# Loads of V, A's K, output weights and x cut into 16 source elements of 16 KB

## The chip, the cores and the metric

One core of a Trainium2 chip, the other cores idle. The metric is the time of one execution on the device in microseconds (us). A run is called slow when it is over 1.5% above the fastest of the same kernel; ratios are of fast runs alone, each made on one chip beside runs of the kernel before. Medians are of all runs of a kernel, and where a slow run is among them the text says so.

A few words: HBM is the chip's main memory, SBUF the core's own memory of 128 partitions. PE, DVE, ACT and POOL are the compute engines. A load (one DMA) is issued by a queue and carried out by 16 DMA engines in packets; the traces show small packets of 4 bytes with it, here called completions (14,112 for the 882 DMAs of the kernel before, 16 each), and the profile gives the time from issue to landing. In these traces a packet is as large as the piece that lies together in HBM (2 to 32 KB in the loads of these runs; the source element, here often called a row).

## The reference

Two attention blocks side by side, in bf16. Both have 16 sequences of 32 query tokens, model width 1024, 32 query heads of 128 and a cache of 1024 keys.

```python
# A: 4 KV heads, each shared by 8 query heads.  B: 32 KV heads, one for each query head.
q = (x @ wq).reshape(B, Sq, Hq, Dh).transpose(0, 2, 1, 3)
scores = einsum("bhqd,bhkd->bhqk", q, k) * Dh ** -0.5
p = softmax(scores)
o = einsum("bhqk,bhkd->bhqd", p, v)
y = o.transpose(0, 2, 1, 3).reshape(B, Sq, Hq * Dh) @ wo        # for A and for B
return concatenate([yA, yB], -1)
```

The caches of B are 128 MB each for K and V, those of A 16 MB each; the weights are 8 MB each. Nothing is read twice, so with x (1 MB each) 322 MB must come from HBM once; these are MB of 2^20 bytes, the profile counts them as 338 MB of 10^6.

## The kernel before

The work runs in 128 steps. Each loads one group of four B heads (1 MB of K in one DMA, 1 MB of V in four) and, every second step, one head of A's K and V (256 KB each). All DMAs are issued from one queue, that of SyncE (SP), in an order fixed ahead by a list scheduler in the kernel. Buffers are few (2 for B's K, 3 for B's V), so SP waits for a buffer and then refills it.

The four kinds of load that matter:

```python
def folded_load(e, dst, src):          # source and destination may have different shapes
    inst = ...(ins=e.lower_ap_dma(src), outs=e.lower_ap_dma(dst))     # one DMA, from SP's queue
    return e.add_instruction(inst)

# B's K: 128 rows of 8 KB to 128 partitions of 8 KB
ksrc = pb["k"][q.b, q.h0:q.h0 + 4].rearrange("a (p s) d -> (a p) (s d)", s=32)
e.dma_start(KB_sb[:, sl, :, :].rearrange("p i n -> p (i n)"), ksrc)

# B's V, one head: 32 source rows of 8 KB, each to 4 partitions of 2 KB
vsrc = pb["v"][q.b, q.h0 + t_].rearrange("(g p c) d -> g (p c d)", p=4, c=NCH)
folded_load(e, VB_sb[:, sl, t_, :, :].rearrange("p c d -> p (c d)"), vsrc)

# A's K (A's V, the output weights of one head, and x likewise): 128 rows of 2 KB to 128 partitions of 2 KB
e.dma_start(KA_sb[:, sl, :, :], pa["k"][q.b, q.s].rearrange("(p c) d -> p c d", c=NCH))

# projection weights: 2 x 128 pieces of 2 KB
e.dma_start(dst[:, k_ * jp:(k_ + 1) * jp, :], wq[...].rearrange("(j p) c -> p j c", p=P))
# ... compute, scheduler and stores left out
```

## Time and profile before

| | before |
|---|---|
| median of 3 runs, us | 850.37 (848.38 to 855.56) |
| span of the profiled run, us | 849.6 |
| PE / DVE / ACT busy | 85% / 64% / 53% |
| DMA, mean | 402 GB/s |

The page of the kernel before: the slice rows have 40 equal parts of the span, DMA is the busy share of the 16 DMA engines in tenths, GB/s what they moved. In the queue table come packets, MB and share of 16 engines' time. The last rows give the count of DMAs, KB of each, and median us from issue to landing.

```profile
span 849.6 us, 27817 instructions
...
DMA  9999999999999999999999999999999999999995
GB/s 346 384 389 404 410 397 398 414 403 391 411 414 417 417 409 415 414 382 403 419 414 415 412 417 418 409 411 417 419 420 415 407 417 419 408 390 410 418 413 195
DMA packets 82075, 341.59 MB, mean 402 GB/s; under 512 B 14112, under 2 KB 14624, under 8 KB 49184
...
q1 hardware_dynamic: 81952, 339.80, 99.3%
...
DMA 48%; PE 28%; DVE 12%; SPq 6%; issue 3%; ACT 2%; POOL 0%; POOLq 0%; DVEq 0%
...
KB_sb<-in_B_k_cache_dram SPq DMA_DIRECT2D x128, 1024.0 KB, 8.6
VB_sb<-in_B_v_cache_dram SPq DMA_DIRECT2D x512, 256.0 KB, 8.5
```

The DMA engines are busy nearly all the time (99.3%) and move some 415 to 420 GB/s in the good slices. The row before the last two is the chain that ended last: nearly half of it is DMA. The packet counts are cumulative: 14,112 small ones are the completions (16 for each of 882 DMAs), 34,560 have 2 KB, and the remaining 32,891 have 8 KB and more, among them 16,384 of B's K and 16,384 of B's V.

Who waits, in the kernel before (us in total, times, longest us):

```profile
DVE KBt_sb L844 <- DMA KB_sb<-in_B_k_cache_dram: 62.6, 67, 3.3
...
PE ps_o L971 <- DMA VB_sb<-in_B_v_cache_dram: 29.5, 27, 3.3
...
SPq L809 <- DVE KBt_sb L844: 101.2, 36, 7.7
```

The first two rows are compute that waits for data: little, for 850 us. The last is the issuing queue that waits for a free K buffer.

The packet records of the trace give each packet's duration: 84 ns (median) for 2 KB, 309 for 8 KB, 9 for a completion.

### The profile page before, as it was taken

How to read it: one execution, taken by the hardware profiler on the slowest of the kernel's cores; microseconds unless marked ns; L12 is line 12 of the kernel's file. 1: busy time of each engine (PE TensorE's matmuls, PEld its weight loads, DVE VectorE, ACT ScalarE, POOL GpSimd, SP SyncE). 2: the span in 40 equal slices, each digit the busy share in tenths (PEclk: the TensorE clock that was granted, in tenths of full speed). 3: DMA queues.
4: the chain of work that ended last, by engine and by line, in shares of the span. 5: the costliest groups of instructions: out<-in, count | busy, mean ns of one | idle time of the engine just before them, and what ended most of it. 6: DMA issues, size and time to landing. Idle time of an engine off the chain costs nothing.

```text
span 849.6 us, 27817 instructions
## 1 busy us (share of the span) xinstructions
PE 722.7 (85%) x12104; PEld 430.9 (51%) x12104; DVE 544.4 (64%) x1117; ACT 448.5 (53%) x981; POOL 68.2 (8%) x76
## 2 busy tenths in 40 slices
PE   3999999799988799789988788987999867877777
PEld 2556655456545455445654445553655544544443
DVE  0655676467755677457785566775677756757854
ACT  1455666366644466445655445754565635555453
POOL 0000000000000000000000000000000000000000
PEclk9999999999999999989999999999999989999999
DMA  9999999999999999999999999999999999999995
GB/s 346 384 389 404 410 397 398 414 403 391 411 414 417 417 409 415 414 382 403 419 414 415 412 417 418 409 411 417 419 420 415 407 417 419 408 390 410 418 413 195
DMA packets 82075, 341.59 MB, mean 402 GB/s; under 512 B 14112, under 2 KB 14624, under 8 KB 49184
## 3 DMA queue, kind: packets, MB, share of 16 engines
q1 hardware_dynamic: 81952, 339.80, 99.3%
q8 instruction: 96, 1.57, 0.7%
q14 instruction: 27, 0.22, 0.1%
HBM read 337.64 MB, written 2.10 MB: 400 GB/s over the span
## 4 chain that ended last, share of the span: by engine, by line
DMA 48%; PE 28%; DVE 12%; SPq 6%; issue 3%; ACT 2%; POOL 0%; POOLq 0%; DVEq 0%
DMA KB_sb<-in_B_k_cache_dram 28%; DVE KBt_sb L844 9%; DMA VB_sb<-in_B_v_cache_dram 8%; PE ps_pj L674 7%; DMA woB_sb<-in_B_wo_dram 6%; PE ps_s L879 5%; DMA VA_sb<-in_A_v_cache_dram 4%; SPq L498 4%; PE ps_pj L731 4%; PE ps_o L971 3%; PE ps_kt L937 2%; PE ps_pt L921 2%; PE ps_s L862 2%; DMA KA_sb<-in_A_k_cache_dram 1%; DMA acc<-in_B_x_dram 1%
## 5 line engine op out<-in xcount | busy, mean ns | idle before, releaser
L844 DVE STREAM_TRANSPOSE KBt_sb<-KB_sb 128x1024 f32<-128x1024 f32 x256 | 306.4, 1226 | 70.6 <-DMA KB_sb<-in_B_k_cache_dram 62.6
L902 ACT ACTIVATE P_sb<-ps_s 128x512 bf16<-128x512 f32 x256 | 151.8, 598 | 84.7 <-PE ps_s L879 73.7
L894 ACT ACTIVATE PTA_sb<-ps_s 128x1024 bf16<-128x1024 f32 x128 | 131.6, 1028 | 91.6 <-PE ps_s L862 73.7
L879 PE MATMUL ps_s<-KBt_sb,QB_sb 32*32 32x512 bf16 x4096 | 144.1, 388 | 9.4 <-DVE KBt_sb L844 4.6
L674 PE MATMUL ps_pj<-xT_sb,wq_sb 128*128 128x512 bf16 x448 | 121.0, 385 | 14.1 <-DMA wq_sb<-in_B_wq_dram 4.6
L818 POOL COPY VAp_sb<-VA_sb 128x1024 bf16<-128x1024 bf16 x64 | 66.7, 1042 | 762.3 <-DMA VA_sb<-in_A_v_cache_dram 735.8
L604 ACT COPY PT_sb<-ps_pt 128x512 f32<-128x512 f32 x128 | 75.0, 586 | 97.9 <-PE ps_o L971 80.6
L971 PE MATMUL ps_o<-VB_sb,PT_sb 128*32 128x128 bf16 x4096 | 82.3, 222 | 34.0 <-DMA VB_sb<-in_B_v_cache_dram 29.5
L921 PE MATMUL ps_pt<-id,P_sb 128*128 128x128 f32 x512 | 100.1, 302 | 8.5 <-ACT P_sb L902 5.7
L971 PEld LDWEIGHTS ps_o<-VB_sb,PT_sb 128*32 128x32 bf16 x4096 | 60.4, 97 | 71.4 <-issue 66.3
L921 PEld LDWEIGHTS ps_pt<-id,P_sb 128*128 128x128 f32 x512 | 79.4, 206 | 27.7 <-ACT P_sb L902 10.2
L862 PE MATMUL ps_s<-QT_sb,KTA_sb 128*128 128x256 bf16 x512 | 84.0, 275 | 7.3 <-ACT PTA_sb L894 5.1
L937 PE MATMUL ps_kt<-VAp_sb,PTA_sb 128*128 128x129 bf16 x1024 | 76.4, 221 | 7.9 <-ACT KTA_sb L604 2.6
L987 DVE TENSOR_SCALAR OB_sb<-ps_o,rinv_all 128x128 bf16<-128x128 f32 x128 | 44.0, 344 | 58.6 <-PE ps_o L971 57.2
L937 PEld LDWEIGHTS ps_kt<-VAp_sb,PTA_sb 128*128 128x128 bf16 x1024 | 64.4, 98 | 33.5 <-POOL VAp_sb L818 12.9
L879 PEld LDWEIGHTS ps_s<-KBt_sb,QB_sb 32*32 32x32 bf16 x4096 | 49.1, 89 | 62.2 <-issue 9.8
L731 PE MATMUL ps_pj<-woB_sb,OTB_sb 128*128 128x512 bf16 x240 | 68.2, 390 | 7.5 <-DMA woB_sb<-in_B_wo_dram 5.2
L674 PEld LDWEIGHTS ps_pj<-xT_sb,wq_sb 128*128 128x128 bf16 x448 | 40.3, 108 | 50.2 <-DMA wq_sb<-in_B_wq_dram 7.7
L742 DVE TENSOR_TENSOR acc<-acc,ps_pj 128x512 f32<-128x512 f32 x64 | 43.0, 672 | 30.4 <-PE ps_pj L731 30.2
L731 PE MATMUL ps_pj<-woA_sb,OTA_sb 128*128 128x512 bf16 x224 | 57.1, 379 | 3.7 <-DMA woA_sb<-in_A_wo_dram 1.9
L862 PEld LDWEIGHTS ps_s<-QT_sb,KTA_sb 128*128 128x128 bf16 x512 | 44.9, 98 | 29.0 <-ACT PTA_sb L894 9.1
L907 DVE TENSOR_TENSOR stat<-stat 64x1 f32<-64x1 f32 x256 | 41.9, 164 | 18.2 <-ACT P_sb L902 10.2
(52 smaller groups left out, 521.6 us busy)
## 6 DMA issues: line engine op xcount, KB each, us to landing
KB_sb<-in_B_k_cache_dram SPq DMA_DIRECT2D x128, 1024.0 KB, 8.6
VB_sb<-in_B_v_cache_dram SPq DMA_DIRECT2D x512, 256.0 KB, 8.5
KA_sb<-in_A_k_cache_dram SPq DMA_DIRECT2D x64, 256.0 KB, 9.2
VA_sb<-in_A_v_cache_dram SPq DMA_DIRECT2D x64, 256.0 KB, 8.8
wq_sb<-in_B_wq_dram SPq DMA_DIRECT2D x16, 512.0 KB, 10.3
woB_sb<-in_B_wo_dram SPq DMA_DIRECT2D x32, 256.0 KB, 9.8
woA_sb<-in_A_wo_dram SPq DMA_DIRECT2D x32, 256.0 KB, 8.7
wq_sb<-in_A_wq_dram SPq DMA_DIRECT2D x12, 512.0 KB, 10.0
```

Of the source, the lines that this page charges most:

```text
L604: pr.add("act", lambda e: e.copy(dst_ap, src_ap), reads=reads, writes=writes, name=name + "@act", wtag=wtag, rtag=rtag)
L674: last = e.matmul(ps_pj[:, 0:NTOK], pick(src, j), xT_sb[:, pi, j, :], start=(j == 0), stop=(j == DJ - 1))
L731: last = e.matmul(ps_a[:, 0:OUTW], OT[:, gp, hh, :], wo_[:, hh, oh * OUTW:(oh + 1) * OUTW], start=(hh == 0), stop=(hh == nh - 1))
L818: pr.add("pool", lambda g: g.tensor_copy(VAp_sb[:, sl, :, 0:Dh], VA_sb[:, :, :]), reads=["VA"], writes=[("VAp", sl)], name="VAp_cp", rtag= ...
L844: pr.add("dve", lambda e: e.transpose(KBt_sb[:, sl, t_, :].bitcast(F32).rearrange("p (s r i) -> p s r i", r=2, i=32), KB_sb[:, rs, t_, :]. ...
L862: last = e.matmul(ps_s[:, sbf, c2, i * 2 * P:(i + 1) * 2 * P], KTA_sb[:, sl, c * P:(c + 1) * P], qt, start=True, stop=True)
L879: last = e.matmul(ps_s[32 * cg:32 * cg + 32, sbf, g, :].rearrange("p (sh cl j) -> p sh cl j", sh=4, cl=4), lhsT, kt[32 * a:32 * a + 32, g, ...
L894: pr.add("act", lambda e: e.activation(dst, src, ACTF.Exp, scale=scale), writes=BK_S[sbf] + [("PTA", q.half)], name="expA", rtag={("Sv", s ...
L902: pr.add("act", lambda e, src=src, dst=dst, g=g: e.activation(dst, src, ACTF.Exp, scale=scale, accum_out=st[:, g:g + 1]), writes=[BK_S[sbf ...
L921: last = e.transpose(ps_pt32[:, m * P:(m + 1) * P], p32[:, m:Sk // 2:NPK], id32[:])
L937: last = e.matmul(ps_kt[:, qh * OA0:qh * OA0 + Dh + 1], PTA_sb[:, h, c, qh * P:(qh + 1) * P], VAp_sb[:, sl, 4 * h + c, 0:Dh + 1], start=(h ...
L971: last = e.matmul(ps_o[32 * a:32 * a + 32, 0:Dh], PT_pairs[:, c // 2, 32 * (a ^ (c // 4 * 2)):32 * (a ^ (c // 4 * 2)) + 32, c % 2], VB_sb[ ...
```

## The change

The intent: by estimate from the durations above a DMA packet has a fixed cost (5 ns, the remainder of 84 ns for 2 KB and 309 for 8 KB when what grows with the bytes and an overlap of 4 ns are taken off), so fewer and larger packets should move the same bytes in less time. Each 256 KB load becomes 16 source rows of 16 KB, so that each of the 16 DMA engines should get one packet. A row of 16 KB then fills 8 partitions of 2 KB.

```diff
-def folded_load(e, dst, src):
+def wide_load(e, dst, src, groups=16):
     ...
-        ins=e.lower_ap_dma(src), outs=e.lower_ap_dma(dst))
+        ins=e.lower_ap_dma(src.rearrange("(g n) d -> g (n d)", g=groups)), outs=e.lower_ap_dma(dst))
     return e.add_instruction(inst)
@@ x, output weights of A and of B, A's K, A's V: all in this way
-                e.dma_start(KA_sb[:, sl, :, :], pa["k"][q.b, q.s].rearrange("(p c) d -> p c d", c=NCH))
+                wide_load(e, KA_sb[:, sl, :, :].rearrange("p c d -> p (c d)"), pa["k"][q.b, q.s])
@@ B's V
-                    vsrc = pb["v"][q.b, q.h0 + t_].rearrange("(g p c) d -> g (p c d)", p=4, c=NCH)
-                    folded_load(e, VB_sb[:, sl, t_, :, :].rearrange("p c d -> p (c d)"), vsrc)
+                    vsrc = pb["v"][q.b, q.h0 + t_]
+                    wide_load(e, VB_sb[:, sl, t_, :, :].rearrange("p c d -> p (c d)"), vsrc)
```

B's K (8 KB packets) and the projection weights (2 KB) are not touched.

More of the change, by code (lines that the diff above doesn't have):

```diff
@@ L611, in xT_stage @@
             for tc in range(NG):
-                pr.add("sp", lambda e, tc=tc: e.dma_start(xst[:, tc, :], xfs[pi][tc * P:(tc + 1) * P, :]),
+                pr.add("sp", lambda e, tc=tc: wide_load(e, xst[:, tc, :], xfs[pi][tc * P:(tc + 1) * P, :]),
                        writes=accres if tc == 0 else [("xst", pi, tc)], reads=[] if tc == 0 else accres, dma_key=f"x{pi}_{tc}", name="x_dma", dur=P * D * 2)
@@ L700, in th @@
                 def th(h_=h_, r0=r0):
-                    pr.add("sp", lambda e: e.dma_start(woA_sb[:, h_, :], wo[r0:r0 + Dh, :]),
+                    pr.add("sp", lambda e: wide_load(e, woA_sb[:, h_, :], wo[r0:r0 + Dh, :]),
                            writes=[("woA", h_)], dma_key=f"woA{h_}", name="woA_dma", dur=Dh * D * 2, wtag={("woA", h_): s_})
@@ L710, in th @@
                 def th(h_=h_, r0=r0):
-                    pr.add("sp", lambda e: e.dma_start(woB_sb[:, h_, :], wo[r0:r0 + Dh, :]),
+                    pr.add("sp", lambda e: wide_load(e, woB_sb[:, h_, :], wo[r0:r0 + Dh, :]),
                            writes=[("woB", h_)], dma_key=f"woB{h_}", name="woB_dma", dur=Dh * D * 2, wtag={("woB", h_): m_})
@@ L803, in st_dmaK @@
                 sl = q.kvslot
-                pr.add("sp", lambda e: e.dma_start(KA_sb[:, sl, :, :], pa["k"][q.b, q.s].rearrange("(p c) d -> p c d", c=NCH)),
+                pr.add("sp", lambda e: wide_load(e, KA_sb[:, sl, :, :].rearrange("p c d -> p (c d)"), pa["k"][q.b, q.s]),
                        writes=[("KA", sl)], dma_key=f"ka{sl}", name="ka_dma", dur=Sk * Dh * 2, wtag={("KA", sl): q.kid})
@@ L815, in st_dmaV @@
                 sl = q.kvslot
-                pr.add("sp", lambda e: e.dma_start(VA_sb[:, :, :], pa["v"][q.b, q.s].rearrange("(p c) d -> p c d", c=NCH)),
+                pr.add("sp", lambda e: wide_load(e, VA_sb[:, :, :].rearrange("p c d -> p (c d)"), pa["v"][q.b, q.s]),
                        writes=["VA"], dma_key="va", name="va_dma", dur=Sk * Dh * 2, wtag={"VA": q.kid})
@@ L822, in st_dmaV @@
                 for t_ in range(4):
-                    vsrc = pb["v"][q.b, q.h0 + t_].rearrange("(g p c) d -> g (p c d)", p=4, c=NCH)
-                    pr.add("sp", lambda e, t_=t_, vsrc=vsrc: folded_load(e, VB_sb[:, sl, t_, :, :].rearrange("p c d -> p (c d)"), vsrc), writes=[("VB", sl, t_)],
+                    vsrc = pb["v"][q.b, q.h0 + t_]
+                    pr.add("sp", lambda e, t_=t_, vsrc=vsrc: wide_load(e, VB_sb[:, sl, t_, :, :].rearrange("p c d -> p (c d)"), vsrc), writes=[("VB", sl, t_)],
                            dma_key=f"vb{sl}_{t_}", name="vb_dma", dur=Sk * Dh * 2, wtag={("VB", sl, t_): q.kid})
```

## The prediction

> **What bounds the kernel now.** The DMA engines. DMA is at 9 tenths in 39 of 40 slices, the queue table gives the hardware queue 99.3% of 16 engines' span, at a mean of 402 GB/s. PE is busy 85%, DVE 64%, ACT 53%. The chain of waits is 48% DMA (B's K alone 28%), 28% PE, 12% DVE. Good slices run at 415 to 420 GB/s, poor ones at 380 to 400, where loads wait for buffers (waits of the issuing queue: 101 us on B's K transposes).
>
> **Where DMA time goes.** The packet records of the trace have three common durations: 84 ns for 2 KB (34,560 packets), 309 ns for 8 KB (32,768: half B's K, half B's V, already loaded in 8 KB source elements) and 9 ns for each 4-byte completion (14,112). Successive packets of one engine mostly overlap by 4 ns, so a packet costs about 80, 305 and 5 ns: 0.0366 ns per byte and 5 ns per packet. Summed over 16 engines this makes 803 us of 849.6; the rest is stretched packets (about 20 us), gaps, start and tail.
>
> **What the change does.** Instruction order, bytes, buffers and the count of DMAs stay. A load of 256 KB becomes 16 source elements of 16 KB, one per DMA engine. B's V: 16,384 packets of 8 KB to 8,192 of 16 KB. A's K and V, both output weights, x: 25,600 of 2 KB to 3,200 of 16 KB. Packets fall from 81,952 to about 51,360.
>
> Estimate from the durations above (16 KB: 605 ns effective, about 609 recorded): B's V saves 8,192 x 5 ns / 16 = 2.6 us; the 2 KB loads save (25,600 x 80 - 3,200 x 605) / 16 = 7.0 us. Together 9.6 us, 1.1%. [...]the trace agrees with a small fixed cost, here 5 ns, so most of it is already gone at 8 KB.
>
> **How much is on the critical path.** Nearly all in good slices, little in poor ones, where compute returns buffers late. I expect 60 to 100%: 6 to 9.6 us. Issuing a reshaped load takes 594 ns (B's V) against 432 ns for an ordinary one of the same size (timeline); some 200 such issues add 30 us, hidden behind 8 us of queued loads.
>
> **Prediction.** 842 us, 8 in 10 between 831 and 851. Faster by over 2%: 0.11; within 2%: 0.83; slower by over 2%: 0.06.
>
> **What the profile would show.** Packets near 51,400, almost all 2 KB packets left belonging to the projection weights; 16 KB packets at about 609 ns; good slices at 420 to 427 GB/s; PE, DVE and ACT busy times unchanged; poor slices still poor; DMA share still 97 to 99%.
>
> **What would make it wrong.** (a) Contention at SBUF: a 16 KB element spans 8 partitions[...]. No trace here shows it; then 16 KB packets would last well over 609 ns and the kernel would be slower. (b) Fewer packets may also shrink the stretched packets and gaps (about 36 us): then over 2% faster. (c) The issuing queue becomes the limit through dearer issues. (d) Compute absorbs all of the gain.

The sum came to 2.6 + 7.0 = 9.6 us, of which 60 to 100% were expected to arrive, hence 842 us. Point (a) says that an element of 16 KB spans 8 partitions; why that should cost time was not shown.

## The result, and the profile after

| | before | after |
|---|---|---|
| median, us | 850.96 (4 runs) | 1253.87 (4 runs, 1244.52 to 1294.56, the last slow) |
| ratio of fast runs | | 1.469 (1.452 to 1.486) |
| profiled span, us | 849.6 | 1242.7 |
| DVE / ACT busy, us | 544.4 / 448.5 | 550.3 / 452.7 |
| PE busy, us | 722.7 | 828.6 |
| granted TensorE clock, share of full | 0.986 | 0.844 |

A ratio is the mean time of one kernel's fast runs over that of the other's of the same rounds, so it is not quite the ratio of the medians quoted. The median of the three fast runs of the changed kernel is 1245.26 us, 394 above the kernel before.

The page of the changed kernel, the same rows (it has 123 instructions fewer because that many matmul records are missing from this trace):

```profile
span 1242.7 us, 27694 instructions
...
DMA  9999999999998999989999999899999999989996
GB/s 328 296 296 274 322 262 269 272 269 269 280 264 246 276 266 263 278 251 265 270 292 282 256 285 262 236 289 291 266 290 286 280 306 286 284 258 283 289 276 183
DMA packets 51483, 341.59 MB, mean 275 GB/s; under 512 B 14112, under 2 KB 14624, under 8 KB 23584
...
q1 hardware_dynamic: 51360, 339.80, 96.1%
...
DMA 72%; DVE 9%; SPq 8%; PE 7%; issue 2%; ACT 0%; POOL 0%; POOLq 0%; DVEq 0%
...
KB_sb<-in_B_k_cache_dram SPq DMA_DIRECT2D x128, 1024.0 KB, 14.1
VB_sb<-in_B_v_cache_dram SPq DMA_DIRECT2D x512, 256.0 KB, 14.9
```

The DMA engines are as busy as before, 9 tenths nearly everywhere, yet move only 275 GB/s in place of 402. Busy engines at a lower rate mean here that packets last longer (B's K 432 ns against 309, below), not that loads are missing. The DMA share of the queue (96.1% after, 99.3% before) hardly tells the two kernels apart; the GB/s row beside it does. The chain is now 72% DMA.

Who waits after the change:

```profile
DVE KBt_sb L845 <- DMA KB_sb<-in_B_k_cache_dram: 293.1, 105, 7.7
...
PE ps_o L972 <- DMA VB_sb<-in_B_v_cache_dram: 147.4, 62, 6.1
...
SPq L810 <- DVE KBt_sb L845: 160.2, 33, 11.3
```

Compute waits for data nearly five times as long as before, also for B's K, whose load was not changed.

The packet records tell where the time went. The last two columns are the sum of the durations over 16 engines, in us:

| packets | median ns before | median ns after | mean ns after | us before | us after |
|---|---|---|---|---|---|
| 16 KB (changed loads) | – | 958 | 948 | – | 674.6 |
| 8 KB, B's K | 309 | 432 | 436 | about 325 (half of 649.8) | 446.3 |
| 8 KB, B's V | 309 | – | – | about 325 | – |
| 2 KB | 84 | 98 | 108 | 184.8 | 60.5 |
| completions | 9 | 13 | 13.4 | 8.0 | 11.8 |

Altogether 844.0 us of packets became 1194.8 (with the output stores' 1.5 in both). So 351 of the 393 us by which the spans differ lie in longer packets, the rest in gaps. 16 KB packets last 948 ns where 609 were expected, and the untouched packets of B's K last 40% longer (median 432 ns against 309). This points to something that all loads share. That a load gives each engine one packet fits the trace: the 16 packets of the first load, a part of B's x, are all under way at once (the last starts 0.32 us after the first, and they last 702 to 1064 ns).

The clock of TensorE fell too. It is not the cause of the long packets: the loads alone, below, show them with the granted clock at 1.00 in every stage.

### The profile page after: what moved, and what is told of

Same layout as the page of the kernel before. It is cut to its first block, busy times and chain, and to the rows that moved or that the text cites. A ratio compares the mean times of both kernels' runs of the same rounds, so it can differ in the third digit from the quotient of the medians.

```text
span 1242.7 us, 27694 instructions
## 1 busy us (share of the span) xinstructions
PE 828.6 (67%) x11981; PEld 478.1 (38%) x12104; DVE 550.3 (44%) x1117; ACT 452.7 (36%) x981; POOL 68.0 (5%) x76
## 3 DMA queue, kind: packets, MB, share of 16 engines
q1 hardware_dynamic: 51360, 339.80, 96.1%
## 4 chain that ended last, share of the span: by engine, by line
DMA 72%; DVE 9%; SPq 8%; PE 7%; issue 2%; ACT 0%; POOL 0%; POOLq 0%; DVEq 0%
DMA KB_sb<-in_B_k_cache_dram 48%; DMA VB_sb<-in_B_v_cache_dram 10%; DVE KBt_sb L845 8%; SPq L499 7%; DMA VA_sb<-in_A_v_cache_dram 5%; DMA woB_sb<-in_B_wo_dram 3%; DMA KA_sb<-in_A_k_cache_dram 3%; PE ps_pj L675 2%; PE ps_s L880 1%; DMA woA_sb<-in_A_wo_dram 1%; DMA out_dram<-ost 1%; PE ps_pj L732 1%; PE ps_o L972 1%; DMA acc<-in_B_x_dram 1%; SPq L810 1%
## 5 line engine op out<-in xcount | busy, mean ns | idle before, releaser
L972 PE MATMUL ps_o<-VB_sb,PT_sb 128*32 128x128 bf16 x4096 | 94.4, 243 | 148.9 <-DMA VB_sb<-in_B_v_cache_dram 147.4
L880 PE MATMUL ps_s<-KBt_sb,QB_sb 32*32 32x512 bf16 x4096 | 175.1, 460 | 19.1 <-DVE KBt_sb L845 12.8
L675 PE MATMUL ps_pj<-xT_sb,wq_sb 128*128 128x512 bf16 x408 | 130.2, 432 | 40.0 <-DMA wq_sb<-in_B_wq_dram 12.9
L972 PEld LDWEIGHTS ps_o<-VB_sb,PT_sb 128*32 128x32 bf16 x4096 | 71.0, 107 | 191.1 <-issue 185.3
L922 PE MATMUL ps_pt<-id,P_sb 128*128 128x128 f32 x512 | 110.1, 327 | 7.4 <-ACT P_sb L903 4.7
L938 PE MATMUL ps_kt<-VAp_sb,PTA_sb 128*128 128x129 bf16 x1024 | 88.0, 241 | 25.9 <-POOL VAp_sb L819 19.1
L938 PEld LDWEIGHTS ps_kt<-VAp_sb,PTA_sb 128*128 128x128 bf16 x1024 | 74.7, 109 | 60.6 <-POOL VAp_sb L819 36.7
L836 PE MATMUL ps_kt<-ident,KA_sb 128*128 128x128 bf16 x512 | 48.0, 248 | 58.0 <-DMA KA_sb<-in_A_k_cache_dram 57.7
L605 ACT COPY OTB_sb<-ps_o 128x128 bf16<-128x128 bf16 x128 | 34.1, 266 | 96.6 <-PE ps_o L993 95.8
L836 PEld LDWEIGHTS ps_kt<-ident,KA_sb 128*128 128x128 bf16 x512 | 36.9, 112 | 76.9 <-DMA KA_sb<-in_A_k_cache_dram 69.8
```

The source lines that it names most:

```text
L605: pr.add("act", lambda e: e.copy(dst_ap, src_ap), reads=reads, writes=writes, name=name + "@act", wtag=wtag, rtag=rtag)
L675: last = e.matmul(ps_pj[:, 0:NTOK], pick(src, j), xT_sb[:, pi, j, :], start=(j == 0), stop=(j == DJ - 1))
L880: last = e.matmul(ps_s[32 * cg:32 * cg + 32, sbf, g, :].rearrange("p (sh cl j) -> p sh cl j", sh=4, cl=4), lhsT, kt[32 * a:32 * a + 32, g, ...
L922: last = e.transpose(ps_pt32[:, m * P:(m + 1) * P], p32[:, m:Sk // 2:NPK], id32[:])
L938: last = e.matmul(ps_kt[:, qh * OA0:qh * OA0 + Dh + 1], PTA_sb[:, h, c, qh * P:(qh + 1) * P], VAp_sb[:, sl, 4 * h + c, 0:Dh + 1], start=(h ...
L972: last = e.matmul(ps_o[32 * a:32 * a + 32, 0:Dh], PT_pairs[:, c // 2, 32 * (a ^ (c // 4 * 2)):32 * (a ^ (c // 4 * 2)) + 32, c % 2], VB_sb[ ...
```

## The experiments

The theories:

- **P, place in SBUF.** How long a packet lasts depends on which partitions are written at the same time: some writes of different engines get into each other's way. With 16 rows a row covers 8 neighbouring partitions, with 32 rows 4. This is a supposition that the runs below test. A mechanism behind it was not shown.
- **S, size.** A source element of 16 KB is slow by itself, at HBM or in the DMA engine.
- **I, issue.** Reshaped loads are too dear to issue.

### Loads alone

No compute: 15 stages of one form of load each, 16 MB a stage (8 MB in the last two), with a wait for all of them between stages. The stages read the same bytes of B's V cache (the last two the first half of them). The list is abridged:

```diff
+("plain2k",                uniform, 256 KB, 128 rows of 2 KB)
+("rows32_8k_4part",        uniform, 256 KB, 32 rows of 8 KB)
+("rows16_16k_8part",       uniform, 256 KB, 16 rows of 16 KB)
+("k_plain8k",              uniform, 1 MB, 128 rows of 8 KB)
+("k_rows64_16k_2part",     uniform, 1 MB, 64 rows of 16 KB)
+("rows32_16k_4part",       uniform, 512 KB, 32 rows of 16 KB to 4 partitions of 4 KB each)
+# then "mix_k_...": 1 MB in B's K form and 1 MB in the form named, in turn
+# rows16x2: 16 rows of two pieces of 8 KB that do not touch in HBM; a piece fills 4 partitions
+# half_64part: partitions 0 to 63 alone; step2_64part: every second one of 128
```

> Loads without any compute, 15 stages of 16 MB (the last two of 8 MB), one form of load per stage; the output is wrong on purpose. [...] Expected: 16 rows of 16 KB on 8 partitions each clearly below the 32-row form of the same bytes, most so mixed with B's K form, about 270 to 330 GB/s against 415 to 430; 32 rows of 16 KB on 4 partitions (4 KB each) at about 609 ns a packet and over 415 GB/s, mixed or not; 64 rows of 16 KB on 2 partitions likewise; 16 rows of 8 KB on 8 partitions (1 KB each), mixed with K, stretched to 400 ns or more, while 32 rows of 4 KB on 4 partitions, mixed, stay at about 157 ns. 64 partitions 0 to 63 alone: about half the rate[...]. Theory S (size of the source element: HBM side or the engine's own handling of 16 KB): every form with 16 KB elements near 950 ns a packet however many partitions it fills, and 16 rows of 8 KB at 309 ns. Theory I (issue): the 16-row form is limited by issue, with packets near 609 ns and gaps between them.

The figures up to those of theory S are what theory P expects.

Measured in windows, one for each stage in the order of the table below (columns: stretch and length in us, then the busy engines, the granted clock, DMA share and GB/s):

```profile
0.73:48.31 47.58, 0.00 (x0) 1.00 0.98 353
48.33:95.65 47.32, 0.00 (x0) 1.00 0.95 355
95.67:150.59 54.92, 0.00 (x0) 1.00 0.97 306
150.60:193.48 42.88, 0.00 (x0) 1.00 0.95 391
193.50:235.88 42.38, 0.00 (x0) 1.00 0.95 396
235.90:280.39 44.49, 0.00 (x0) 1.00 0.95 377
280.40:325.40 45.00, 0.00 (x0) 1.00 0.94 373
325.42:382.69 57.27, 0.00 (x0) 1.00 0.96 293
382.71:425.79 43.08, 0.00 (x0) 1.00 0.95 389
425.81:476.60 50.79, 0.00 (x0) 1.00 0.97 330
476.62:530.97 54.35, 0.00 (x0) 1.00 0.86 309
530.99:602.44 71.45, 0.00 (x0) 1.00 0.98 235
602.46:659.82 57.36, 0.00 (x0) 1.00 0.97 293
659.84:702.74 42.90, 0.00 (x0) 1.00 0.95 196
702.75:726.04 23.29, 0.00 (x0) 1.00 0.90 360
```

Read across stages: the DMA share differs little (0.94 to 0.98, but for one stage of 4 KB packets and the short last one), the last column does.

| stage | GB/s | packets of the form, median ns | partitions of one element |
|---|---|---|---|
| plain2k | 353 | 2 KB: 86 | 1 |
| rows32_8k_4part | 355 | 8 KB: 336 | 4 |
| rows16_16k_8part | 306 | 16 KB: 812 | 8 |
| k_plain8k | 391 | 8 KB: 309 | 1 |
| k_rows64_16k_2part | 396 | 16 KB: 622 | 2 |
| rows32_16k_4part | 377 | 16 KB: 640 | 4 |
| mix_k_rows32_8k_4part | 373 | 8 KB, both kinds: 321 | 4 |
| mix_k_rows16_16k_8part | 293 | 16 KB: 1042; K's 8 KB: 314, mean 354 | 8 |
| mix_k_rows32_16k_4part | 389 | 16 KB: 640; K's 8 KB: 314, mean 318 | 4 |
| mix_k_rows16_8k_8part | 330 | 8 KB, both kinds: 368 | 8 |
| mix_k_rows32_4k_4part | 309 | 4 KB: 159 | 4 |
| rows16x2_8k_4part | 235 | 8 KB: 541 | 4 |
| mix_k_rows16x2_8k_4part | 293 | 8 KB, both kinds: 465 | 4 |
| half_64part_8k | 196 | 8 KB: 638 | 1 |
| step2_64part_8k | 360 | 8 KB: 309 | 1 |

What follows:

- Theory S falls. Elements of 16 KB on 4 or on 2 partitions last 640 and 622 ns, alone or beside K, close to the 609 expected. Only those on 8 partitions are slow (812 and 1042).
- Size is not needed either: 8 KB elements in 16 rows (mixed) stretch, though less than expected (368 ns for both kinds together, 400 or more expected).
- The stage rows16x2 refines theory P. Its packets are of the size and the form that B's V has in the kernel before, 8 KB on 4 partitions. But a row holds two of them that lie side by side. It is the slowest of the forms that fill 128 partitions: 235 GB/s and 541 ns, against 355 and 336 for 32 rows and 391 and 309 for B's K. So it is not the span of one element that hurts. Theory P's reading is that it matters which partitions are written at the same time; which are, the packet records do not tell.
- Writing only the first 64 partitions halves the rate too (196 against 391), while every second one of 128 does not (360): 638 against 309 ns a packet. That agrees with theory P: the number of partitions is 64 in both, only their places differ.
- The rates of these stages are below the expected 415 to 430 even in the good forms (353 to 396). A stage of 256 KB loads has an issue of 590 to 600 ns for each and a start and a landing of its own; that this is the reason is the author's estimate. The packet durations are the better reading. The mixed stage with 4 KB packets may be slow partly for that reason (its DMA share was 0.86); its medians are 159 and 309 ns, but the means 182 and 359, so part of its packets were long as well.

### 32 rows in place of 16, everywhere

```diff
-def wide_load(e, dst, src, groups=16):
+def wide_load(e, dst, src, groups=32):
```

> The change with one number altered: 32 source elements of 8 KB (4 partitions each) in place of 16 of 16 KB (8 partitions each), for the same six loads. Theory P: [...]packets of 8 KB back at 309 ns, time 840 to 848, ratio to before 0.985 to 0.998. Theory S: the same. Theory I (reshaped loads are dear to issue): issue times stay those of the change, about 590 ns each, so the time stays well over 1,000. A theory that blames the contiguous reshaping of the small loads as such expects the same.

Measured: 852.2 us, ratio to before 1.002 (0.999 to 1.006), result right. Packets of 8 KB are back at 309 ns.

```profile
span 851.0 us, 27817 instructions
...
DMA packets 62875, 341.59 MB, mean 401 GB/s; under 512 B 14112, under 2 KB 14624, under 8 KB 23584
```

The single number 16 to 32 takes away the whole loss. Theory I falls as the cause of it: these loads take about as long to issue as in the changed kernel (B's V 638 against 679 ns, A's V 627 against 745), and the time is that of before. But the miss is instructive as well: 19,200 packets fewer, 6 us of fixed cost by the estimate of 5 ns each, and nothing gained. The sum of packet durations did fall, from 844.0 to 838.9 us; the span did not. What the span has beyond that sum merely grew, from 5.6 to 12.1 us. More on that below.

### The change in two parts

```diff
 # the kernel before, with B's V alone in 16 rows:
-folded_load(e, VB_sb[...], vsrc)       # 32 rows of 8 KB
+wide_load(e, VB_sb[...], vsrc)         # 16 rows of 16 KB
```

> The kernel before with B's V alone changed to 16 elements of 16 KB (8 partitions each): 128 of the 178.4 MB of the change. If the loss goes with the bytes in wide form, 72% of 403 us: about 1,140 us, ratio 1.34. B's K packets of 8 KB, untouched, stretched over 400 ns under theory P[...] and, if HBM were the limit, too; under a cost inside the engine that moves the wide packet they stay at 309.

Measured: 1194.44 and 1204.16 us in the two fast runs, ratio 1.411 (1.404 to 1.418); the other two were slow (1223.26 and 1238.05). The profile is of a slow run, so only the fast times are used for the size of the effect. In that profile K's packets, untouched, have a median of 424 ns, so neighbours are slowed as in the whole change (432).

```diff
 # the change, with B's V left in 32 rows:
-wide_load(e, VB_sb[...], vsrc)
+wide_load(e, VB_sb[...], vsrc, groups=32)
```

> The rest of the change alone: A's K and V, output weights and x in 16 elements of 16 KB, B's V as before in 32 of 8 KB: about 50 of 178 MB. By bytes, 28% of 403 us: about 965 us, ratio 1.13. Under theory P with stretched neighbours somewhat more, up to 1,000.

Measured: 1027.01 us, ratio 1.207 (1.201 to 1.212). K and V packets of 8 KB average 373 ns (before 317), those of 16 KB 926.

The two parts cost 41% and 21%, together 47%. The loss does not go with the bytes in wide form: 28% of them give 44% of the loss. A reading that fits, argued and not tested: 16-row loads also stretch the packets beside them (here those of 8 KB from 317 to 373 ns), so the first wide loads do most harm. The split by bytes was wrong for both.

### The packets of before, in 16 rows

```diff
-vsrc = pb["v"][q.b, q.h0 + t_].rearrange("(g p c) d -> g (p c d)", p=4, c=NCH)
-folded_load(e, VB_sb[:, sl, t_, :, :].rearrange("p c d -> p (c d)"), vsrc)
+vsrc = pb["v"][q.b, q.h0 + t_].rearrange("(h g p c) d -> g h (p c d)", h=2, p=4, c=NCH)
+folded_load(e, VB_sb[:, sl, t_, :, :].rearrange("p (a c) d -> p a (c d)", a=2), vsrc)
```

> The kernel before with one thing changed for B's V: the same 256 KB as 16 rows of two separate pieces of 8 KB, so packets stay 8 KB, each still fills 4 partitions[...], and their number stays; but one row[...] now covers 8 neighbouring partitions, as in the change. The order of keys is wrong on purpose. Theory P[...]: as bad as B's V alone in 16 KB form or worse, 1,200 us and more, V packets of 8 KB at 430 to 560 ns in place of 309. Theory S (source elements of 16 KB) or a theory that the span of one element over 8 partitions costs by itself: 850, packets at 309.

Measured: 1224.24 us, ratio 1.437 (1.432 to 1.443). 8 KB packets, V's and K's together, have a median of 469 ns.

```profile
span 1222.2 us, 27817 instructions
...
DMA packets 82075, 341.59 MB, mean 279 GB/s; under 512 B 14112, under 2 KB 14624, under 8 KB 49184
```

The packet row is that of the kernel before to the last packet; the rate is that of the changed kernel. So neither the size nor the number of packets, nor the span of an element, is needed for the loss. What this run shares with the change is the 16 rows, each of which covers 8 neighbouring partitions. Its pieces of 1 KB in a partition (2 KB before) get a control of their own below. One reservation: these loads also issue slowly here (1209 ns on average, median 609). The issuing queue as the cause is unlikely, because it still waited 379 us for buffers and the packets themselves were stretched. And one warning: the comparison with the reference passed, though the keys of V are misplaced within each head. So it did not catch this order of keys with these inputs.

### 16 KB packets on 4 partitions

```diff
-for t_ in range(4):
-    vsrc = pb["v"][q.b, q.h0 + t_].rearrange("(g p c) d -> g (p c d)", p=4, c=NCH)
-    folded_load(e, VB_sb[:, sl, t_, :, :]..., vsrc)
+for t_ in (0, 2):
+    vsrc = pb["v"][q.b, q.h0 + t_:q.h0 + t_ + 2] # as 32 rows of 16 KB
+    folded_load(e, VB_sb[:, sl, t_:t_ + 2, :, :].rearrange("p t c d -> p (t c d)"), vsrc)
```

> The kernel before with B's V in loads of 512 KB for two heads: 32 source elements of 16 KB, each on 4 partitions of 4 KB[...]. The places of the keys are wrong on purpose. Same packets of 16 KB as the change gives V, other partitions. Theory P: 16 KB packets at 609 to 640 ns, K at 309, time 838 to 852, ratio 0.985 to 1.002. Theory S: packets near 950 ns, about 1,200 us as in the run with V alone in 16 rows.

Measured: 840.97 us, ratio 0.987 (0.983 to 0.990); result wrong. 16 KB packets: median 611 ns, mean 618; 8 KB: 309.

```profile
DMA packets 69783, 341.53 MB, mean 406 GB/s; under 512 B 10016, under 2 KB 10528, under 8 KB 45088
```

This is the counterpart of the run with V alone in 16 rows: the same 8,192 packets of 16 KB, the same bytes, other partitions (and half as many issues for V), and 841 us in place of 1,194 and 1,204. The duration that the prediction gave a 16 KB packet, 609 ns, is right for this form.

### B's K in 16 KB elements

```diff
-ksrc = pb["k"][q.b, q.h0:q.h0 + 4].rearrange("a (p s) d -> (a p) (s d)", s=32)
-e.dma_start(KB_sb[...], ksrc)
+ksrc = pb["k"][q.b, q.h0:q.h0 + 4].rearrange("a (p s) d -> (a p) (s d)", s=64)
+folded_load(e, KB_sb[...], ksrc)
```

> The kernel before with B's K, which the change left alone, in 64 source elements of 16 KB, each on 2 partitions of 8 KB[...]; right result. Theory P: no collision, packets at about 609 to 622 ns; 8,192 packets' fixed cost of 5 ns less, 2.6 us of DMA time, of which the run with 32 rows everywhere (0.7% expected, nothing seen) suggests that little arrives: 846 to 852, ratio 0.995 to 1.003. Theory S: 50% slower like the change.

Measured: 856.7 us, ratio 1.004 (1.000 to 1.008), just outside the expectation's upper end. Packets of 16 KB: median 611 ns, mean 638. The packets are not stretched as in the change, and there is no gain: the packet records add to 846.1 us (before 844.0), so the saving did not even appear there. An issue of K also took 524 ns on average in place of 409; whether that cost anything was not separated.

### Partitions alone

Loads alone again. The first six stages are ordinary loads of 8 KB a partition and differ only in which partitions they fill.

```diff
+("p128_all",  slice(0, 128)), ("p32_first", slice(0, 32)),    ("p32_step4", slice(0, 125, 4)),
+("p32_step2", slice(0, 63, 2)), ("p16_step4", slice(0, 61, 4)), ("p16_step8", slice(0, 121, 8)),
+# then 256 KB loads: rows32x2, rows16x2, rows32, rows16, rows8, rows64; K in 64 rows mixed with rows32 and rows16
```

> Loads alone again, 14 stages. The first six are ordinary loads of 8 KB a partition that differ only in which partitions they fill: all 128; 0 to 31; every fourth of 128 (32 of them); every second of the first 64 (32); every fourth of the first 64 (16); every eighth of 128 (16). Theory P[...] those two have packets at 309 ns, the other four about double, 600 to 640[...]. Then 256 KB loads: 32 rows of two 4 KB pieces (2 partitions each, written as 1 KB pieces) at about 159 ns, which shows that the 1 KB pieces of the pairing run are harmless; 16 rows of two 8 KB pieces near 541 again; 32 rows near 309 to 340, 16 rows near 812 again; 8 rows of 32 KB use at most 8 engines, so 220 GB/s or less; 64 rows of 4 KB on 2 partitions near 159. Last two: B's K form in 64 rows of 16 KB mixed with 32 rows (over 370 GB/s) and with 16 rows (below 310).

"Those two" are all 128 and every fourth of 128. A figure of about double was at hand from the first run: 638 ns for partitions 0 to 63 alone.

The windows of the first four stages, and of the later stages with 32 and with 16 rows:

```profile
0.73:43.18 42.45, 0.00 (x0) 1.00 0.96 395
43.20:65.78 22.58, 0.00 (x0) 1.00 0.90 186
65.79:80.57 14.78, 0.00 (x0) 1.00 0.79 284
80.59:103.13 22.54, 0.00 (x0) 1.00 0.91 186
...
249.42:296.70 47.28, 0.00 (x0) 1.00 0.95 355
296.71:361.73 65.02, 0.00 (x0) 1.00 0.97 258
```

| partitions, or form | packets, median ns |
|---|---|
| all 128 | 309 |
| 0 to 31 | 638 |
| every fourth of 128 (32) | 309 |
| every second of the first 64 (32) | 641 |
| every fourth of the first 64 (16) | 455 |
| every eighth of 128 (16) | 494 |
| 32 rows of two 4 KB pieces | 191 |
| 16 rows of two 8 KB pieces | 529 |
| 32 rows of 8 KB | 336 |
| 16 rows of 16 KB | 973 |
| 8 rows of 32 KB | 1280 |
| 64 rows of 4 KB | 172 |
| K in 64 rows beside 16 rows of 16 KB | 833 |

The pair to look at is 0 to 31 against every fourth of 128: the same 32 rows of 8 KB, the same packets, the same issue time (590 and 588 ns), and 638 against 309 ns, with a DMA share over 16 engines of 0.90 in the slow one and 0.79 in the fast one. Only the partitions differ, so it is the place in SBUF that doubles the duration. By what mechanism, the trace does not show.

Misses: the two forms with 16 partitions came to 455 and 494, not 600 to 640. Their loads of 128 KB were issued one in 0.63 to 0.65 us, and the DMA share was 0.57 and 0.62, so fewer packets were under way at once; that this is why they were stretched less is an argument, not tested. The control with 1 KB pieces lasted 191 ns, not 159; that is far from the doubling of the 16-row form, but not free. The 16-row form gave 973 ns here and 812 in the run before: how hard it is hit varies.

One form stays unexplained. With 8 rows about half of the engines' time was used (DMA share 0.49, 196 GB/s), and a row covers even 16 neighbouring partitions; yet a packet of 32 KB lasted 1280 ns, about twice the 622 to 640 of an unstretched 16 KB. So a row of many partitions is not enough for a stretch; whether it takes more packets under way at once was not tested.

Mixed with K in 64 rows, the 16-row form gave 313 GB/s, a little over the expected limit of 310; beside 32 rows, 379.

### Where the saved packets' time went

32 rows everywhere saved 6 us on paper and nothing on the clock, yet V in loads of 512 KB won 10 us, of which its packets explain some 4 (8,192 packets and 4,096 completions fewer, at the estimated 5 ns, over 16 engines). That run also halves the issues for V. The issuing queue of the kernel before spends 503 us issuing 882 DMAs (the sum of their issue times in the trace) and 347 us waiting, together the span; so it issues or waits all the time.

```diff
-vsrc = ... as 32 rows of 16 KB      # loads of 512 KB, as in the run on 4 partitions
+vsrc = ... as 64 rows of 8 KB
```

> Where did the 6 us go that 32 rows everywhere should have saved, and why did the run with V in loads of 512 KB gain 10 us where packets account for some 4? As that run (V of two heads in one load, 256 issues for V in place of 512, keys misplaced on purpose), but in 64 source elements of 8 KB on 2 partitions each: the packets are those of the kernel before in size and number, only the issues are halved. If the issuing queue is the second limit (it issues or waits all of the time: 503 and 347 us of 850): 841 to 845, ratio 0.987 to 0.993, issue total near 330 us. If the 16 KB packets made the gain: 848 to 851, ratio 0.998 to 1.002.

Measured: 841.52 us, ratio 0.990 (0.987 to 0.994); wrong result. The issues add to 331 us.

```profile
DMA packets 77975, 341.53 MB, mean 407 GB/s; under 512 B 10016, under 2 KB 10528, under 8 KB 45088
```

The data packets are those of before in size and number, and most of the gain is there. The interval overlaps that of the 16 KB packets (0.983 to 0.990), so at most a few tenths of a per cent are theirs. But this run did not halve the issues alone: a row now fills 2 partitions of 4 KB in place of 4 of 2 KB, and a load holds two heads. And the packet records add to 835.7 us in place of 844.0: 2.3 us less for completions, 6.4 less for the 8 KB packets, whose mean is 314 ns in place of 317. So most of the gain (8.4 of the 10.5 us by which the spans differ) is in the packets' own time, and none of it needs larger packets; how much comes from fewer issues, and how much from the other form, is not shown.

```diff
 # 32 rows for A's K and V and x; output weights ordinary again, two heads to a load:
-wide_load(e, woA_sb[:, h_, :], wo[r0:r0 + Dh, :])
+e.dma_start(woA_sb[:, h_:h_ + 2, :], wo[r0:r0 + 2 * Dh, :].rearrange("(h p) c -> p h c", p=P))
```

> An attempt at a correct kernel that beats both: A's K and V and x in 32 rows of 8 KB, output weights as ordinary loads again, but two heads to a load (512 KB, 2 KB elements), so 32 issues for them in place of 64. DMA time falls by some 4 us against before, issue time stays about that of before (+25 us of dearer issues, -16 us of saved ones). If issue is the second limit: 845 to 851, ratio 0.993 to 1.000; if only packets counted: 844 to 847.

Measured: 853.9 us, ratio 1.006 (1.002 to 1.010); right result. A miss: packets add to 837.8 us (before 844.0), issues to 511 us (before 503), and the time rose a little. So neither a sum of packet time nor a sum of issue time explains the small differences of these kernels.

## Why the prediction was wrong

**Right.** DMA bounds the kernel; the order stays; packets fell to exactly 51,360; 8,960 packets of 2 KB remain, nearly all those of the projection weights (8,192); busy times of DVE and ACT hardly changed. (That of PE was also expected to stay; it rose from 722.7 to 828.6 us at the lower clock.) The estimated fixed cost of about 5 ns per packet is consistent with the 611 ns that 16 KB lasted on 4 partitions.

**The step that failed.** "Estimate from the durations above (16 KB: 605 ns effective, about 609 recorded)". The line through 2 KB and 8 KB was drawn from loads of 32 and 128 rows, and used for a form of 16 rows whose packets do not lie on it. 16 KB packets lasted 948 ns on average. The same step took for granted that the packets of B's K stay at 309; they rose to 432 (median). Those two terms, 675 us against an expected 434 (11,392 packets of 609 ns over 16 engines) and 446 against 325, are nearly the whole loss.

**A cause of this kind was named and set aside.** Point (a) of the prediction, contention at SBUF, gives the sign and what the packets would show: packets well over 609 ns and a slower kernel. It is followed by "No trace here shows it", and all of "slower by over 2%" got a chance of 6%. The traces could not show it: in the kernel before no load has that form. Missing evidence should not have counted as evidence against. The finer point was wrong too: (a) blames an element that spans 8 partitions. The run with the packets of before and 16 rows shows nearly the same loss (ratio 1.437) with elements on 4 partitions each.

**Rather what happens.** Loads of 128, 64 and 32 source rows kept their packets short here: 309 to 336 ns for 8 KB (alone, or as the median in the kernel). Loads of 16 rows did not: 812 and 973 ns for 16 KB alone, 958 in the kernel, where 611 to 640 were measured on 4 partitions. Which engine writes which partitions, and where writes of two engines get into each other's way, no trace shows, since the packet records do not name the engine or the partition. Two things are shown: that the rows make the difference, with packets and bytes held still (1,224 against 851 us), and that packets last twice as long when a load fills partitions 0 to 31 in place of every fourth of 128 (638 against 309 ns). That the first is a case of the second is argued, and the form with 8 rows is not explained by it.

**"I expect 60 to 100%" of the saving failed too.** With the stretch out of the way (32 rows), 5 us of packet time were saved and none of it arrived. Point (c), the issuing queue as a second limit, is left open: the run with half of V's issues gained 1%, but mostly in packet time and with another form, and the last run missed.

## What to carry to other kernels

Before a load is cut into fewer, larger source rows, ask how many neighbouring partitions one source row will cover: with 32 rows or more for 128 partitions the packets kept their duration (309 ns for 8 KB in the kernel), with 16 they did not (958 ns for 16 KB, where 611 were measured on 4 partitions), and the time went from 852 to 1,245 us (fast runs) for that one number. A packet cost read from one form of load need not hold for another form; a stage of some 50 us of loads alone on the chip shows it before the kernel is touched. When the DMA share stays at 9 tenths and GB/s falls (402 to 275 here), look at the packet durations, also those of loads that were not changed.
